# Moving seven pieces of w2 and the last turns of wq to later steps of a backward pass

## The chip, the cores and the metric

The kernel runs on one core of a Trainium2 chip. Its time is the device time of one execution in microseconds (us); three runs were timed, and their median is the figure compared. One more execution was recorded by the hardware profiler, and every duration below comes from that record.

The core has engines that work side by side and each take their own instructions in order: PE multiplies matrices (PEld loads its weights), DVE and ACT work on vectors, POOL does so too and issues some transfers, and SP here only issues transfers (DMAs). Sixteen DMA engines move the bytes between the chip's memory and the core's own.

## What is computed

Two transformer layers with the same weights, one token per sequence, two sequences, forward and backward. Each layer is an attention block over a cached K and V (4 heads of K and V, 16384 positions, 128 wide; 32 heads of queries) and an MLP with a layer norm in front of each:

```python
x = x + _A_ref(_layernorm(x), A_k_cache, A_v_cache, A_wq, A_wo)   # attention, layer 0
x = x + _B_ref(_layernorm(x), B_w1, B_b1, B_w2, B_b2)             # MLP, layer 0
x = x + _A_ref(_layernorm(x), A_k_cache, A_v_cache, A_wq, A_wo)   # attention, layer 1
x = x + _B_ref(_layernorm(x), B_w1, B_b1, B_w2, B_b2)             # MLP, layer 1
...
_out, _vjp = jax.vjp(_f, A_x, A_k_cache, A_v_cache, A_wq, A_wo, B_w1, B_b1, B_w2, B_b2)
_grads = _vjp(grad_out)
return (_out0, *[jnp.asarray(_g) for _g in _grads])
```

In the attention `q = x @ wq`, the scores are softmaxed, `o = p @ v`, and the result is `o @ wo`. In the MLP `y = _layernorm(x)`, `h = gelu(y @ w1 + b1)`, and the result is `h @ w2 + b2`. The outputs are the last x (`out_0`) and the gradients of x, of both caches (32 MB each, in bfloat16), of the four weights and of the two biases. w2 is 3584 x 1024.

## The kernel before

**The list of pieces.** The program isn't written engine by engine. Each small piece of work is a Python function that is put on one list with `emit`, together with the chunks of memory that it uses. At the end `Program.run` (L109) walks through the list in order and calls the functions; every engine then has its instructions in exactly that order. So the place of a piece in the list is its place in the order of each engine that it touches.

**Chunks and slots.** Whatever is loaded comes in chunks of up to 1 MB (128 partitions x 4096 numbers of 2 bytes), one DMA on SP each. Sixteen tiles called `slot`, and for a time a few others (halves of `e`, `ds` and `late`), hold chunks. `run` places chunks in the order of their first use, as soon as a slot is free that fits, often a dozen pieces ahead; a chunk keeps its slot until the last piece that uses it. SP issues its DMAs in that same order, and each waits until the slot's last user is done. A chunk may also be a scratch area of the program, without a load. `Program.keep` (L79) decides which chunks stay in their slot between two uses; after that there are 338 loads.

**The backward pass of layer 1.** `attn_bwd` (L1048) goes over the eight pairs of sequence and K/V head in order, 16 steps for each, 128 steps in all, and 14 more (`LAG_B`), in which only what lags behind is left. A step s does this:

- DVE turns a quarter of a V chunk (`kblock`, L554), and PE multiplies it with the gradient (L567), two steps later in the list. A chunk of V so lasts four steps.
- PE multiplies a quarter of a K chunk, 14 steps behind V's (`direct`, called as `pk`; L592), so the last K chunks are used at steps 126 to 141.
- Twice in 16 steps DVE makes the scores' gradient (`slope`, L1067 and L1070) and ACT and POOL exchange its parts (`exchange`, L602).
- Then come the pieces in `wb` and `extra` for that step.

`wb` holds the weights of the attention: wo's next group, and wq's group of the head just finished. The last group of wq is turned at steps 118 to 125, and its products (`tail`) come when the pass is over. To turn a piece in place (`turn_here`, L451), PE transposes eight blocks of 128 x 128 into PSUM (L457) and ACT copies them back over the piece (L460). `here_products` (L466, PE at L470) multiplies a turned piece.

`extra` holds the MLP's w2, which layer 1's forward result and layer 0's backward pass both need. It is loaded once, in seven chunks (pieces) of 512 rows. `w2_fwd_piece` (L892, PE at L896) makes 32 products with a piece as it was loaded, and then four `turn_here` turn it in place. It keeps its slot until the pass is over, when `here_products` uses it for layer 0. After the seventh piece `x_out` (L1451, two DVE additions) finishes x, and `col_to_row` (L626) makes it `out_0`: two PE transposes (L633), a DVE copy into a scratch chunk that lies in a load slot (L634), and a DMA of 4 KB on POOL (L635).

**After the pass**, in this order: the first of the transposes on DVE that turn w1 for layer 0 (`turn_rows`, L442), the eight products of the last wq group, the backward pass of the layer norm (`attn_in_bwd`, L1187; on DVE from L672 on, with one PE product at L683), more turns of w1, and the 28 products of w2 (L470). Their result is needed by everything of layer 0. Layer 0's backward pass also makes and stores the large outputs.

The lines around the change:

Of the kernel before, what the change touches and what calls it, by code (L numbers as in the profile page):

```python
# [182 lines left out]
def kernel(  # L183
# [70 lines left out]
    def ob():  # L254
        st["ob"] += 1
        return obanks[st["ob"] % len(obanks)]
# [139 lines left out]
    def ld_w2():  # L396
        return [ld_rows("w2", B_w2, 4 * i, 4, 0, D) for i in range(FJ // 4)]

    def col(c, j, n, o):
        return c.ap[:, j * n + o * 128:j * n + (o + 1) * 128]  # L400
# [83 lines left out]
    def turned_products(ps, t, w0, nw, vb, first, last, parts=1):  # L484

        def f(k):
            def fn():
                tv = t.ap[:, 0:nw * 256].rearrange("p (w x e) -> p w x e", x=128, e=2)
                for w in range(k * nw // parts, (k + 1) * nw // parts):
                    for e in range(2):  # L490
                        J = (w0 + w) // 2
                        PE.matmul(ps(), lhsT=tv[:, w, :, e], rhs=vb()[:, 2 * (w % 2) + e, :, 2 * J:2 * J + 2],
                                  start=(first and w == 0 and e == 0), stop=(last and w == nw - 1 and e == 1),
                                  skip_group_check=True)
            return fn

        return [(f(k), [t]) for k in range(parts)]
# [128 lines left out]
    def col_to_row(colT, dram_out, queue=None, kind="half"):  # L626
        c = P.chunk(kind=kind)

        def f():
            row = c.ap[0:DJ, 0:256].rearrange("p (b n) -> p b n", b=2)  # L630
            ps = ob()[0:DJ, 0:256].rearrange("p (b n) -> p b n", b=2)
            for b in range(2):
                PE.transpose(ps[:, b, :], colT[:, :, b], identf[:])  # L633
            V.tensor_copy(out=row, in_=ps)  # L634
            (queue or GP).dma_start(dram_out.rearrange("b (j n) -> j b n", n=128), row)  # L635

        return f, [c]
# [254 lines left out]
    def w2_fwd_piece(l, ws, i, fps):  # L892
        def f():
            for j in range(4):
                for o in range(DJ):
                    PE.matmul(fps[:, o, :], lhsT=col(ws[i], j, 1024, o), rhs=h_all[:, 4 * i + j, 2 * l:2 * l + 2],  # L896
                              start=False, stop=True, skip_group_check=True)
        return f, [ws[i]]
# [79 lines left out]
    def wo_bwd_ops(l, k, vb):  # L978

        acc = sb[0][:, 64:80].rearrange("p (c a b) -> p c a b", c=2, a=4)  # L980

        def fin():
            raw = regroup(acc, ob())
            V.memset(sb[0][:, 64:80], 0.0)
            dve(0.3)
            do_of(l, k, raw)

        return turned_pair(ld_wo(k), acc, vb), (fin, ())
# [10 lines left out]
    def wo_mid_ops(l, k):  # L999

        ws = ld_wo(k)
        ps = sb[0][:, 64:80].rearrange("p (r b) -> p r b", b=2)
        turns = [turn_here(ws[r // 4], (r % 4) * 1024, 8) for r in range(R)]
        prods = [here_products(ws[r // 4], (r % 4) * 1024, 8, lambda r=r: ps[:, r, :],
                               lambda o: gA_all[:, o, 2 * l:2 * l + 2], False) for r in range(R)]

        def fin():
            do_of(l, k, ps)
            V.memset(sb[0][:, 64:80], 0.0)
            dve(0.1)  # L1010

        saved["wo"] = ws
        return turns, prods, (fin, ())
# [13 lines left out]
    def wq_bwd_ops(l, k):  # L1027

        acc = sb[0][:, 96:112].rearrange("p (c a b) -> p c a b", c=2, a=4)
        hold = {}  # L1030

        def sp():
            vb, fn = spread(lambda: dq_all[:, k * R:(k + 1) * R, 2 * l:2 * l + 2], 8, "vg")
            hold["vb"] = vb
            fn()

        return [(sp, ())] + turned_pair(ld_wq(k), acc, lambda: hold["vb"]())

    def wq_last_ops(l, k):

        ws = ld_wq(k)
        ps = sb[0][:, 112:128].rearrange("p (j b) -> p j b", b=2)
        turns = [turn_here(ws[j // 4], (j % 4) * 1024, 8, "act" if l == 1 else None) for j in range(DJ)]
        prods = [here_products(ws[j // 4], (j % 4) * 1024, 8, lambda j=j: ps[:, j, :],
                               lambda r: dq_all[:, k * R + r, 2 * l:2 * l + 2], l == 0) for j in range(DJ)]
        return turns, prods

    def attn_bwd(l, order, gT, wo_first, outputs=None, mark=None, extra=None, after=()):  # L1048
# [9 lines left out]
        ev, wb = {}, {}  # L1058
# [33 lines left out]
        for pos, g in enumerate(order):  # L1092
            quick = l == 0 and pos == G - 1
            for f in range(2):
                n = 117 + 5 * f if quick else 16 * pos + 10 + 8 * f
# [10 lines left out]
        for i, k in enumerate(kvs):  # L1106
            if i + 1 < HKV and l == 1:
                turns, prods, fi = wo_mid_ops(l, kvs[i + 1])
                for n in range(8):
                    wb.setdefault(32 * i + 17 + n, []).append(turns[n])  # L1110
                    wb.setdefault(32 * i + 18 + n, []).append(prods[n])
                wb.setdefault(32 * i + 27, []).append(fi)
                turns, prods = wq_last_ops(l, k)
                for n in range(8):
                    wb.setdefault(32 * i + 24 + LAG_B + n, []).append(turns[n])
                    wb.setdefault(32 * i + 33 + LAG_B + n // 4, []).append(prods[n])
            elif i + 1 < HKV:
                ops, fi = wo_bwd_ops(l, kvs[i + 1], vba)
                for n, b in enumerate(ops + [fi]):
                    wb.setdefault(32 * i + 19 + n, []).append(b)  # L1120
                for n, b in enumerate(wq_bwd_ops(l, k)):
                    wb.setdefault(32 * i + 33 + LAG_B + n, []).append(b)
            else:
                if l == 0:
                    wb.setdefault(32 * i + 12 + LAG_B, []).append((dn_kept, ()))
                ops, tail = wq_last_ops(l, k)
                for n, b in enumerate(ops):
                    wb.setdefault((118 if l == 1 else 121) + n, []).append(b)

        kc, vc = {}, {}  # L1130
        n_steps = 128 + LAG_B if l == 1 else N_END
# [5 lines left out]
        s = 0  # L1137
        while s <= n_steps:
# [16 lines left out]
            n = -(-len(fill) // 3)  # L1155
# [3 lines left out]
            for v in v_at.get(s, ()):  # L1159
                pos, i = divmod(v, 16)  # L1160
# [253 lines left out]
    def mark(name):  # L1414
        def f(n=0):
            marks[name, n] = len(P.ops)
        return f
# [11 lines left out]
    def at_sb0(c0, n):  # L1429
        return sb[0][:, c0:c0 + n]  # L1430
# [20 lines left out]
    def x_out(xn, xT, fps):  # L1451
        V.tensor_tensor(out=xn[:], in0=fps, in1=b2T[:].to_broadcast([128, DJ, 2]), op=ALU.add)
        V.tensor_tensor(out=xn[:], in0=xn[:], in1=xT[:], op=ALU.add)
# [21 lines left out]
    xA1 = attn_fwd(1, down, lambda: xM0, mark("e1"), w1_turns[0:2], tw[5][1] + tw[6][0] + tw[6][1] + [(dh_last_, ())])  # L1475
# [29 lines left out]
    xM1 = vec.tile([128, DJ, 2], F32, name="xM1")  # L1505
    fps1 = at_sb0(288, 16).rearrange("p (j b) -> p j b", b=2)
    ws2b = ld_w2()
    extra = {2: [(lambda: V.memset(fps1, 0.0), ())]}
    for i in range(7):
        extra.setdefault(26 + 13 * i, []).append(w2_fwd_piece(1, ws2b, i, fps1))  # L1510
    extra[106] = [(lambda: x_out(xM1, xA1, fps1), ())]

    ws2c = ws2b
    dhps0 = at_sb0(160, 56).rearrange("p (j b) -> p j b", b=2)
    w2_turns = [turn_here(ws2c[j // 4], (j % 4) * 1024, 8) for j in range(FJ)]
    for n, b in enumerate(w2_turns):
        extra.setdefault(29 + 13 * (n // 4) + 3 * (n % 4), []).append(b)

    ws1c = [ld_rows("w1q", B_w1, 4 * h, 4, cg * 896, 896) for h in range(2) for cg in range(4)]
    dm_0 = quads(at_sb0(224, 16))  # L1520
# [2 lines left out]
    for n, c in enumerate(ws1c):  # L1523
        t = w1t[n // 4][n % 4] if n == 7 else P.chunk()
        t1 += [] if n == 7 else turn_rows(c, t, 896)
        p1 += turned_products(lambda n=n: dm_0[:, n // 4], t, 14 * (n % 4), 14, vh0, n % 4 == 0, n % 4 == 3)
    extra[111] = [col_to_row(xM1, out_0.rearrange("b s d -> (b s) d"), kind="load")]
    attn_bwd(1, up, lambda: saved["g3"], (None, wo_prods), mark=mark("d1"), extra=extra, after=t1[0:1])
    wo_prods0 = wo_first_ops(0, down[0] % HKV, saved["wo"])[2]

# [36 lines left out]
    extra = {4: [(spread_a0, ())]}  # L1567
# [22 lines left out]
    def outputs(s, rest=False):  # L1590
# [16 lines left out]
        return res  # L1607

    attn_bwd(0, down, lambda: saved["g1"], (va0, wo_prods0), outputs=outputs, extra=extra)
    slots = []  # L1610
    for i, t in enumerate(slot_tiles):
# [46 lines left out]
```

## Time and profile before

| | us |
|---|---|
| runs: median (lowest, highest) | 1102.76 (1102.6, 1106.79) |
| the profiled execution: its time | 1105.32 |
| its span, first to last instruction | 1103.5 |
| busy in the span: PE / DVE / ACT / POOL | 815.1 / 754.9 / 486.1 / 177.0 |
| layer 1's backward pass | 442 to 638 |
| moved in the span | 448.07 MB, 406 GB/s |

A line of the profile names an engine, a line of the kernel (L554), an operation and the tiles as out<-in; the number behind it is a duration or a busy time in us. Behind "<-" in square brackets stands how long the engine was idle before, and who ended that wait. "PEclk" and the third last column of a stretch are the share of its full clock that PE was granted. A DMA share of about 1 means that all sixteen DMA engines had packets throughout; it can come out slightly over 1.

### The profile page before, as it was taken

The numbers are of one execution on the slowest core, as the hardware profiler recorded it, in microseconds if no ns is written. First come the engines' busy times: TensorE is split into PE (matmuls) and PEld (weight loads), VectorE is DVE, ScalarE is ACT, GpSimd is POOL, SyncE is SP. The second block draws the span as 40 slices with busy tenths as digits, with TensorE's granted clock in tenths as the row PEclk, the third lists the DMA queues.
The fourth block names the chain that finished last, engine by engine and source line by source line (L and its number), as shares of the span: only waits on it lengthen the run. The fifth ranks groups of instructions, "written<-read, shape, count | busy, mean of one in ns | idle before, by whom it ended". The sixth has DMA issues, their size and how long they took to land. (4 is left out here: it accounts for less than half of the span.)

```text
span 1103.5 us, 34173 instructions
## 1 busy us (share of the span) xinstructions
PE 815.1 (74%) x14717; PEld 606.6 (55%) x14717; DVE 754.9 (68%) x1442; ACT 486.1 (44%) x1101; POOL 177.0 (16%) x550
## 2 busy tenths in 40 slices
PE   5664666457888657788788578887887897798885
PEld 4554565456777556678778564444443443344453
DVE  5864665168888627665646466887786895698874
ACT  0332222101243321245434426776675785577873
POOL 1000000001000000111111101323332332233330
PEclk9999999999999996588967757999897998899997
DMA  9999999999999999999999999999999999999996
GB/s 371 420 423 420 421 425 422 399 403 397 416 423 421 422 420 373 411 417 421 416 421 398 372 375 392 334 396 423 420 420 424 424 420 420 426 421 421 417 424 249
DMA packets 97404, 448.07 MB, mean 406 GB/s; under 512 B 7608, under 2 KB 11214, under 8 KB 58852
## 3 DMA queue, kind: packets, MB, share of 16 engines
q1 hardware_dynamic: 80004, 350.40, 77.9%
q0 software_dynamic: 17248, 95.48, 21.0%
q8 instruction: 115, 1.88, 0.6%
q14 instruction: 37, 0.30, 0.1%
HBM read 347.23 MB, written 98.62 MB: 404 GB/s over the span
## 5 line engine op out<-in xcount | busy, mean ns | idle before, releaser
L554 DVE STREAM_TRANSPOSE kT<-slot 128x512 int32<-128x512 int32 x432 | 292.0, 695 | 114.6 <-PE sc L567 92.0
L567 PE MATMUL sc<-qbd,kT 128*128 128x32 bf16 x4096 | 262.4, 222 | 14.5 <-DVE kT L554 10.2
L567 PEld LDWEIGHTS <-kT 128*128 128x128 bf16 x4096 | 208.4, 115 | 65.8 <-issue 34.2
L276 ACT CAST slot<-sc 128x512 bf16<-128x512 f32 x291 | 165.7, 593 | 81.0 <-PE sc L1337 44.1
L592 PEld LDWEIGHTS <-slot 128*128 128x128 bf16 x3424 | 140.0, 103 | 100.9 <-issue 49.6
L592 PE MATMUL sb<-xt,slot 128*128 128x8 bf16 x3424 | 156.2, 177 | 41.9 <-DMA slot<-in_A_v_cache_dram 22.9
L1277 PE MATMUL sc<-slot,late 128*128 128x512 bf16 x338 | 128.6, 403 | 28.9 <-DVE slot L279 12.6
L279 DVE CAST slot<-sc 128x512 bf16<-128x512 f32 x166 | 111.6, 678 | 25.4 <-PE sc L1277 12.3
L787 ACT ACTIVATE e<-sc 128x512 bf16<-128x512 f32 x32 | 19.0, 597 | 236.3 <-DVE sc L784 168.9
L460 ACT COPY slot<-tp 128x512 int32<-128x512 int32 x92 | 52.7, 587 | 113.6 <-PE tp L457 91.3
L276 ACT CAST slot<-sb 128x512 bf16<-128x512 f32 x139 | 82.3, 592 | 25.1 <-PE sb L1337 13.4
L457 PE MATMUL tp<-ident,slot 128*128 128x128 bf16 x800 | 74.9, 255 | 11.9 <-DMA slot<-in_A_wq_dram 8.9
L1277 PEld LDWEIGHTS <-late 128*128 128x128 bf16 x512 | 44.9, 99 | 64.7 <-issue 52.3
L1337 PE MATMUL sc<-slot,late 128*128 128x512 bf16 x170 | 66.0, 407 | 16.9 <-DVE slot L279 9.6
L602 ACT COPY xt<-e 32x128 int32<-32x128 int32 x256 | 75.6, 295 | 3.9
L1277 PE MATMUL sb<-slot,late 128*128 128x512 bf16 x174 | 70.3, 404 | 9.5 <-DVE slot L279 3.7
L279 DVE CAST slot<-sb 128x512 bf16<-128x512 f32 x88 | 59.7, 678 | 15.9 <-PE sb L1277 7.1
L457 PEld LDWEIGHTS <-slot 128*128 128x128 bf16 x800 | 60.7, 116 | 14.4 <-DMA slot<-in_A_wq_dram 7.3
L442 DVE STREAM_TRANSPOSE slot<-slot 128x1024 int32<-128x1024 int32 (+1 forms) x44 | 51.0, 1184 | 15.6 <-DMA slot<-in_A_wo_dram 7.5
L602 POOL COPY xt<-ds 32x64 int32<-32x64 int32 x128 | 29.7, 232 | 178.6 <-DVE ds L1070 119.8
L662 POOL TENSOR_TENSOR m_rstd<-ln_vpe,neghalf 128x2 f32<-128x2 f32 x2 | 1.4, 720 | 350.3 <-DVE ln_vpe L660 350.3
L602 POOL COPY xt<-late 32x64 int32<-32x64 int32 x240 | 55.5, 231 | 13.1 <-DVE late L1070 1.6
(292 smaller groups left out, 1074.5 us busy)
## 6 DMA issues: line engine op xcount, KB each, us to landing
slot<-in_A_k_cache_dram SPq DMA_DIRECT2D x102, 1024.0 KB, 15.4
slot<-in_A_v_cache_dram SPq DMA_DIRECT2D x100, 1024.0 KB, 17.3
out_dram<-slot POOLq DMA_DIRECT2D x55, 1024.0 KB, 15.1
slot<-in_A_wq_dram SPq DMA_DIRECT2D x26, 1024.0 KB, 17.5
slot<-in_A_wo_dram SPq DMA_DIRECT2D x25, 1024.0 KB, 17.7
out_dram<-slot POOLq DMA_DIRECT2D x40, 512.0 KB, 16.5
slot<-in_B_w_dram SPq DMA_DIRECT2D x21, 896.0 KB, 15.9
slot<-in_B_w_dram SPq DMA_DIRECT2D x12, 1024.0 KB, 13.9
```

Of the source, the lines that this page charges most:

```text
L276: S.copy(out=dst, in_=src)
L279: V.tensor_copy(out=dst, in_=src)
L442: V.transpose(out=t.ap[:, h * nw * 256:(h + 1) * nw * 256].bitcast(I32).rearrange("p (w j m) -> p w j m", j=4, m=32), in_=c.ap[:, 0:4 * nc ...
L457: PE.transpose(tp[:, j * 128:(j + 1) * 128], c.ap[:, off + j * 128:off + (j + 1) * 128], ident[:])
L460: S.copy(out=d.bitcast(I32), in_=tp.bitcast(I32))
L554: V.transpose(out=kT[:].bitcast(I32).rearrange("p (w j m) -> p w j m", w=4, j=4), in_=c.ap[:, (i % 4) * 1024:(i % 4 + 1) * 1024].bitcast(I ...
L567: PE.matmul(sc[:, a0:a0 + 4, :, 2 * (i % 4) + q], lhsT=kv[:, 2 * q + w, :, e], rhs=qbd[:, q_at(g), 2 * w + e], start=(w == 0 and e == 0), ...
L592: PE.matmul(acc, lhsT=c.ap[:, n * 128:(n + 1) * 128], rhs=xv[:, i // 4, t // 2, :, 2 * (i % 4) + t % 2], start=(fresh and i == 0 and t == ...
L602: (GP.tensor_copy if on[t % len(on)] == "g" else S.copy)(out=d[32 * t:32 * t + 32, c0:c0 + cn, j, :], in_=s[32 * j:32 * j + 32, c0:c0 + cn ...
L787: S.activation(out=e_of(l, g)[:, 8 * f:8 * f + 8].rearrange("p a h b -> p h a b"), in_=sc[f][:].rearrange("p h (a b) -> p h a b", b=8), fu ...
L1277: PE.matmul(ps, lhsT=hold["blk"][:, j, :], rhs=flat(qm(w)[:, hf * 4:hf * 4 + 4, :]), start=True, stop=True)
L1337: PE.matmul(ps, lhsT=hold[j // 4 * 4][:, j % 4, :], rhs=Y.ap[:, y_at + c0:y_at + c0 + cn], start=True, stop=True)
```

## The change

The seven pieces of w2 had their products at steps 26, 39, 52, 65, 78, 91 and 104, and each piece's four turns 3, 6, 9 and 12 steps after them. Now the products are at steps 44, 60, 76, 92, 106, 118 and 130, and the turns 2, 4, 6 and 8 steps after them. `x_out` moves from step 106 to 132, `col_to_row` for `out_0` from 111 to 137. The last wq group is turned at steps 126 to 133 instead of 118 to 125. Nothing is added or left out; as chunks are placed by their first use, the order of the loads and the slots that they get follow.

```diff
                 ops, tail = wq_last_ops(l, k)
                 for n, b in enumerate(ops):
-                    wb.setdefault((118 if l == 1 else 121) + n, []).append(b)
+                    wb.setdefault((126 if l == 1 else 121) + n, []).append(b)
...
-    for i in range(7):
-        extra.setdefault(26 + 13 * i, []).append(w2_fwd_piece(1, ws2b, i, fps1))
-    extra[106] = [(lambda: x_out(xM1, xA1, fps1), ())]
+    w2_at = (44, 60, 76, 92, 106, 118, 130)
+    for i, s_ in enumerate(w2_at):
+        extra.setdefault(s_, []).append(w2_fwd_piece(1, ws2b, i, fps1))
+    extra.setdefault(132, []).append((lambda: x_out(xM1, xA1, fps1), ()))
...
-        extra.setdefault(29 + 13 * (n // 4) + 3 * (n % 4), []).append(b)
+        extra.setdefault(w2_at[n // 4] + 2 * (1 + n % 4), []).append(b)
...
-    extra[111] = [col_to_row(xM1, out_0.rearrange("b s d -> (b s) d"), kind="load")]
+    extra[137] = [col_to_row(xM1, out_0.rearrange("b s d -> (b s) d"), kind="load")]
```

## The prediction

> **What bounds the kernel now.** I read first the page's forty slices. The DMA row is at 9 almost throughout, so for most of the span the kernel moves bytes as fast as its queues allow; time can be won or lost only where that row dips, or where a chain of computation makes the transfers wait.
>
> ```profile
> DMA  9999999999999999999999999999999999999996
> GB/s 371 420 423 420 421 425 422 399 403 397 416 423 421 422 420 373 411 417 421 416 421 398 372 375 392 334 396 423 420 420 424 424 420 420 426 421 421 417 424 249
> ```
>
> The change touches layer 1's backward pass (442 to 638 us) and what hangs on its end. So next the busy time by stretches; the last two columns are the DMA engines' share and GB/s.
>
> ```profile
> 442.00:600.00 158.00, 124.58 (x2837) 117.42 (x2835) 96.00 (x187) 65.11 (x175) 24.16 (x104) 0.76 1.02 418
> 600.00:613.00 13.00, 9.62 (x266) 9.13 (x265) 8.96 (x16) 5.42 (x15) 2.54 (x9) 0.89 0.75 270
> 613.00:636.00 23.00, 14.43 (x304) 13.85 (x304) 8.39 (x14) 8.47 (x24) 3.71 (x16) 0.72 1.02 419
> ...
> 646.00:650.00 4.00, 3.03 (x89) 2.83 (x87) 1.80 (x4) 0.00 (x0) 0.00 (x0) 0.50 0.57 169
> 650.00:685.00 35.00, 29.66 (x458) 19.15 (x455) 22.27 (x45) 19.27 (x37) 4.03 (x6) 0.63 1.02 414
> 685.00:720.00 35.00, 30.93 (x327) 15.60 (x327) 30.64 (x50) 26.93 (x52) 13.90 (x43) 0.95 0.89 320
> 720.00:1085.00 365.00, 302.57 (x3693) 163.62 (x3692) 286.89 (x479) 251.10 (x489) 117.36 (x337) 0.92 1.01 419
> ```
>
> The DMA engines are full up to 600, lose 13 x 0.25 = 3.25 us in 600:613, are full again, lose 4 x 0.43 = 1.7 us in 646:650, and 35 x 0.11 = 3.9 us in 685:720, where DVE and PE are busy 31 of 35 us: there computation sets the pace. After 720 the transfers do.
>
> What empties the queues at 600:613? SP's own waits (560 to 740 us) hold this line, and the timeline shows the event:
>
> ```profile
> SPq L383 <- DMA out_dram<-slot: 7.1, 1, 7.1
> ```
>
> ```profile
> 603.99 0.38 PE L633 MATMUL sc<-identf,xM 128*8 128x128 f32 x2
> ...
> 604.46 0.41 DVE L634 CAST slot<-sc 8x256 bf16<-8x256 f32 x1 [1.26 <-PE sc L633]
> ...
> 605.17 0.68 POOL L635 DMA_DIRECT2D out_dram<-slot x1 [9.21 <-DVE slot L634]
> ...
> 610.71 0.38 SPq L383 DMA_DIRECT2D slot<-in_A_wq_dram  x1
> ```
>
> At step 111 the row of out_0 is built in a load slot (PE, DVE) and stored by POOL. The next load on SP, a half of the last wq group, goes into that slot, and waits until the 4 KB store has landed: 605.17 + 5.5 = 610.7. Five more loads stand behind it on SP. That is 2.5 of the 3.25 us; the rest (600 to 602.5) follows from PE's two waits at steps 104 and 106, the first two lines here:
>
> ```profile
> 590.68 0.95 PE L896 MATMUL sb<-h_all,slot 128*128 128x2 bf16 x32 [1.52 <-DMA slot<-in_B_w_dram]
> ...
> 595.75 1.03 PE L457 MATMUL tp<-ident,slot 128*128 128x128 bf16 x8 [1.86 <-DMA slot<-in_A_wq_dram]
> ...
> 597.24 1.90 PE L457 MATMUL tp<-ident,slot 128*128 128x128 bf16 x16
> ...
> 636.76 1.02 PE L592 MATMUL sb<-xt,slot 128*128 128x8 bf16 x32 [1.18 <-DMA slot<-in_A_k_cache_dram]
> ```
>
> The last line is the pass's last K chunk arriving: 636.76. From it the tail runs on DVE:
>
> ```profile
> 637.82 0.18 DVE L1077 TENSOR_SCALAR dq_all<-sb 128x8 bf16<-128x8 f32 x1 [5.38 <-PE sb L592]
> ...
> 638.97 1.11 DVE L442 STREAM_TRANSPOSE slot<-slot 128x896 int32<-128x896 int32 x1 [0.83 <-DMA slot<-in_B_w_dram]
> 640.08 0.17 DVE L672 TENSOR_TENSOR lb_dr<-sb,a_rstd 128x16 f32<-128x16 f32 x1
> ```
>
> The norm's backward begins at 640.08, behind the first transpose of w1, and everything of layer 0 follows from it.
>
> **The change, part by part.** Sums are made against this profiled execution (1105.32 us: span 1103.5 and 1.8 around it; 2.6 above the median of 1102.76). Only differences are used, and put onto the median.
>
> *Loads.* 338 planned loads and their bytes stay. The n-th load is released by the same step's work in both kernels (read from the two programs, loads 181 to 255); only which chunk it brings changes, K and V coming up to three places sooner, w2 11 to 18 places later. No byte is saved, so a gain can come only from the lull of 3.25 us. I take all of it as gone: the wait at 595.75 falls away (its wq half comes three places, 7.5 us, sooner), and SP no longer stops behind out_0. One load of 1 MB is 2.5 us at 419 GB/s. So the last K chunk, the same place in the queue as before, arrives at 636.76 - 3.25 = 633.5; w2's seventh piece, now two places ahead of it, at 628.5. Were nothing of the lull saved, both are 3.25 later.
>
> *PE at the end.* 224 products of w2 and 224 transposes with 28 ACT copies move later, and 64 transposes with 8 copies (wq) by 8 steps; none is added. Up to step 129 they lie beside waits for loads (PE 14.43 of 23 us busy in 613:636): at nothing; without that cover a piece costs 0.95 + 4 x 0.5 to 0.95. But step 130's products of the seventh piece stand in PE's order ahead of all the rest, and cannot start before 628.5. Behind them, up to out_0's transposes at step 137: the products 0.95; seven groups on K (1.02 for four, 0.21 each) 1.5; six turns (three of wq, three of w2); out_0's two transposes 0.39. A turn is 0.95 at the slow clock (597.24: two in 1.90), 0.53 at the fast one (two in 1.06 at 587.21). Sum 6.0 to 8.5; end 634.5 to 637.0. The granted clock was 0.72 in 613:636, in the middle; I take 7.3, so 635.8. ACT's copies (0.59 each, two PSUM banks) keep up beside the one exchange of 2.05; x_out's two DVE additions of about 0.17 are free, since DVE idles 5.38 there.
>
> *out_0's store.* The built order of the changed kernel puts out_0's row into the slot that the first transpose of w1 (L442, DVE) writes next, and that transpose now waits for the store; the norm's backward stands behind it on DVE. From PE's end to the landing: 0.08 + 0.41 + 0.30 to POOL's issue, + 5.5 = 6.3; + 1.11 for the transpose: 7.4. POOL has nothing ahead of it (its last exchange ends about 629). The norm begins at 634.5 + 7.4 = 641.9 to 644.4; mid 643.2. Before: 640.08. So +1.8 to +4.3, mid +3.1. wq's eight product groups (1.85 us on PE, 638.19) end before that.
>
> The store's 5.5 us is one row, taken while the DMA engines were 0.5 to 1.0 busy. [...]
>
> *Behind the norm.* One w1 quarter now takes the slot of w2's first piece and is issued some 2.9 us after the norm begins (was 639.2). It is used 12.5 us after; a load into an empty queue landed in 4.7 (433.9 to 438.6), the page's median for this kind is 15.9 behind a full queue. The queue is dry by then: at nothing, at worst +6. The second lull grows by about 4 us; as computation sets the pace until 720, that costs nothing more, and the +3.1 passes through to the end one for one.
>
> *Bounds.* Below: PE keeps up fully, so that only the chunk before the last (631.0) and 0.85 + 0.39 of PE stand ahead: 632.2 + 7.4 = 639.6, -0.4. Above: the lull isn't saved and the clock is slow: 631.8 + 8.5 + 7.4 = 647.7, +7.6.
>
> **The rivals.**
> *Faster: the lull is the whole of it.* If the first transpose did not have to wait on the store, the tail starts with the last K chunk and the gain is 3.25: 1099.5. It decides if out_0's transposes end by 636.8 - 7.4 = 629.4. For: DVE idles 5.38 us before the tail. Against: the seventh piece itself comes at 628.5, and the store's semaphore is in that transpose's waits. 0.13.
> *Much slower: PE held by its own order.* w2's fifth, sixth and seventh pieces are needed at steps 106, 118 and 130, just as they land; PE can't pass them, falls behind, slots come free late and the lull stays: +7.6, 1110.4. For: PE waited at 590.68 for just such a piece. Against: the loads are released some 12 us ahead. 0.20.
> *The store lands quickly.* At best it has landed when POOL's 0.68 us issue ends: 4.8 less than in my sum, so -1.7: 1101.1. For: 4 KB are a two-hundred-fiftieth of a load's 2.5 us. Against: the only such store took 5.5, and its end fell into an emptying queue; here loads are in flight. 0.10. [...]
> *No effect at the end:* computation's slack in 685:720 (4 of 35 us) swallows the delay: 1102.8 or so. 0.07.
>
> **How the numbers follow.** Forecast +3.1: 1105.9, chance 0.50, with its own range 1104.5 to 1107.1. For 8 in 10 I reach towards both sides: 1100.5 (half of the faster case out) to 1109.5 (half of the much slower out). A measurement of this kernel tells about 0.5% (5.5 us) from no change. Faster by more than that needs more than the whole lull: 0.04. Slower, past 1108.3: most of the 0.20 and a tail of the forecast, less what of that case stays below: 0.20. Within: 0.76.
>
> **What would show it.** Right: 600:613 at a DMA share near 1.0; no SP wait on out_dram there; DVE's L442 after dq_all waiting about 4 us for DMA out_dram; the last K chunk used near 633.5 or soon after (PE late); the norm (L672) at about 643; a longer second lull. Wrong: L442 not waiting for the store, that store landing well under 5.5 us, or PE waiting long at L896 with a lull still in front of it.

## The result and the profile after

The changed kernel is slower by about a third of a per cent: 1108.62 us (median of 22 runs, 1104.04 to 1112.95) against 1105.22 for the kernel before on the same chip (22 runs, 1102.6 to 1108.26). The ratio is 1.0030, its 95% interval 1.0021 to 1.0039, so +3.4 us. The forecast was +3.1 on a base of 1102.76, which is +0.28%. The base itself moved by 2.5 us between the two measurements, which is why the median lies nearer to the upper end of the range than the ratio does.

The profiled execution took 1104.04 us (span 1102.3). It is the shortest of the 22, 4.6 below their median, and shorter than the profiled execution of before (1105.32). What it lacks is found below; for now it shows what happens up to 650 us. First the busy time by stretches, with the granted clock of PE, the DMA engines' share and GB/s at the end of each line.

```profile
600.00:613.00 13.00, 9.98 (x236) 9.49 (x233) 8.76 (x14) 3.69 (x11) 2.53 (x11) 0.67 1.02 420
613.00:636.00 23.00, 18.09 (x388) 17.37 (x386) 6.08 (x14) 12.66 (x31) 3.68 (x14) 0.74 1.00 396
636.00:646.00 10.00, 5.78 (x200) 5.63 (x198) 6.20 (x14) 1.90 (x1) 0.00 (x0) 0.63 0.59 198
646.00:650.00 4.00, 2.24 (x78) 2.10 (x76) 1.25 (x3) 0.00 (x0) 0.15 (x1) 0.50 1.04 377
650.00:685.00 35.00, 31.24 (x474) 20.16 (x474) 23.13 (x47) 19.86 (x38) 4.38 (x7) 0.63 1.02 409
685.00:720.00 35.00, 30.92 (x353) 16.20 (x352) 31.54 (x52) 27.43 (x53) 14.72 (x44) 1.00 0.85 324
```

The lull of 600:613 is gone (share 0.75 before, 1.02 now), and SP's waits no longer hold a line on out_dram. In exchange the second lull has grown: 636:646 has a share of 0.59, which is 4.1 us without transfers, after 1.7 us (in 646:650) before. SP issues a load at 636.33 and the next one only at 642.88; it waits for PE's products behind the norm (two such waits, 10.8 us together, this one 6.1):

```profile
SPq L383 <- PE sb L470: 10.8, 2, 6.1
```

The timeline of the changed kernel shows why the norm, and PE behind it, are no earlier:

```profile
628.22 0.95 PE L896 MATMUL sb<-h_all,late 128*128 128x2 bf16 x32 [1.37 <-DMA late<-in_B_w_dram]
...
633.35 0.38 PE L633 MATMUL sc<-identf,xM 128*8 128x128 f32 x2
```

```profile
633.77 0.41 DVE L634 CAST slot<-sc 8x256 bf16<-8x256 f32 x1 [3.30 <-PE sc L633]
635.04 0.17 DVE L1077 TENSOR_SCALAR dq_all<-sb 128x8 bf16<-128x8 f32 x1 [0.86 <-PE sb L592]
...
639.07 1.11 DVE L442 STREAM_TRANSPOSE slot<-slot 128x896 int32<-128x896 int32 x1 [3.71 <-DMA out_dram<-slot]
```

```profile
634.48 0.68 POOL L635 DMA_DIRECT2D out_dram<-slot  x1 [5.02 <-PE tp L457]
```

PE waits for w2's seventh piece until 628.22 and then works without a gap; out_0's row comes out at 633.35, POOL sends its store off at 634.48, and DVE's first transpose of w1 stands 3.71 us until that store has landed at 639.07. The norm's backward follows at 640.10 (640.08 before).

### The profile page after: what moved, and what is told of

Read it like the earlier page. It is cut to its first block, busy times and chain, and to the rows that moved or that the text cites. A ratio compares the mean times of both kernels' runs of the same rounds, so it can differ in the third digit from the quotient of the medians.

```text
span 1102.3 us, 34166 instructions
## 1 busy us (share of the span) xinstructions
PE 824.2 (75%) x14717; PEld 615.7 (56%) x14717; DVE 753.9 (68%) x1442; ACT 487.0 (44%) x1101; POOL 176.1 (16%) x550
## 5 line engine op out<-in xcount | busy, mean ns | idle before, releaser
L567 PE MATMUL sc<-qbd,kT 128*128 128x32 bf16 x4096 | 268.5, 224 | 14.8 <-DVE kT L554 11.1
L567 PEld LDWEIGHTS <-kT 128*128 128x128 bf16 x4096 | 213.2, 117 | 63.2 <-issue 31.4
L592 PE MATMUL sb<-xt,slot 128*128 128x8 bf16 x3488 | 160.4, 177 | 42.4 <-DMA slot<-in_A_v_cache_dram 24.5
L460 ACT COPY slot<-tp 128x512 int32<-128x512 int32 x84 | 48.6, 586 | 103.8 <-PE tp L457 87.8
L457 PE MATMUL tp<-ident,slot 128*128 128x128 bf16 x736 | 72.6, 261 | 2.2 <-DMA slot<-in_A_wq_dram 1.7
L442 DVE STREAM_TRANSPOSE slot<-slot 128x1024 int32<-128x1024 int32 (+1 forms) x46 | 52.7, 1178 | 15.3 <-DMA slot<-in_A_wq_dram 5.9
```

The lines of the kernel that those rows point to most:

```text
L442: V.transpose(out=t.ap[:, h * nw * 256:(h + 1) * nw * 256].bitcast(I32).rearrange("p (w j m) -> p w j m", j=4, m=32), in_=c.ap[:, 0:4 * nc ...
L457: PE.transpose(tp[:, j * 128:(j + 1) * 128], c.ap[:, off + j * 128:off + (j + 1) * 128], ident[:])
L460: S.copy(out=d.bitcast(I32), in_=tp.bitcast(I32))
L567: PE.matmul(sc[:, a0:a0 + 4, :, 2 * (i % 4) + q], lhsT=kv[:, 2 * q + w, :, e], rhs=qbd[:, q_at(g), 2 * w + e], start=(w == 0 and e == 0), ...
L592: PE.matmul(acc, lhsT=c.ap[:, n * 128:(n + 1) * 128], rhs=xv[:, i // 4, t // 2, :, 2 * (i % 4) + t % 2], start=(fresh and i == 0 and t == ...
```

## The experiments

All ratios are to the kernel before, run beside each kernel on the same chip. Where the row is built "in the corner", a small function of its own replaces `col_to_row`; it makes the same row in an unused corner of the long-lived tile `late`, so that no load slot is tied to the store. In these kernels the function shifts what follows by 12 lines (L684 there is L672 here, L1089 is L1077):

```diff
+            row = Lt[0:8, 4096:4352].rearrange("p (b n) -> p b n", b=2)
+            ps = ob()[0:DJ, 0:256].rearrange("p (b n) -> p b n", b=2)
+            for b in range(2):
+                PE.transpose(ps[:, b, :], colT[:, :, b], identf[:])
+            V.tensor_copy(out=row, in_=ps)
+            GP.dma_start(dram_out.rearrange("b (j n) -> j b n", n=128), row)
```

### The wait for the store, taken out of the changed kernel

```diff
-    extra[137] = [col_to_row(xM1, out_0.rearrange("b s d -> (b s) d"), kind="load")]
+    extra[137] = [col_to_row_own(xM1, out_0.rearrange("b s d -> (b s) d"))]
```

> The changed kernel with one edit: out_0's row is built in a corner of the tile late (columns 4096 to 4351) that nothing else uses in this pass, instead of a load slot, so no load and no transpose waits for the store. Store theory (the transpose of w1 that stands ahead of the norm on DVE waits for out_0's store): the changed kernel's 3.71 us wait goes, the norm then follows wq's products, about 2.8 us sooner; ratio to the kernel before 0.997 to 1.000, and no DVE wait for out_dram. Rival (PE is held by w2's late pieces, the wait on the store is only where the delay shows): the time stays that of the changed kernel, 1.002 to 1.004.

1103.86 us, ratio 0.9991 (0.9979 to 1.0002). Against 1.0030 (and 1.0040 for the changed kernel in its second measurement, below) taking the store out of the load slot is worth 0.4 to 0.5%, 4.3 to 5.4 us. DVE's lines in this kernel:

```profile
636.58 0.41 DVE L646 CAST late<-sc 8x256 bf16<-8x256 f32 x1 [4.54 <-PE sc L645]
637.85 0.18 DVE L1089 TENSOR_SCALAR dq_all<-sb 128x8 bf16<-128x8 f32 x1 [0.86 <-PE sb L592]
638.10 0.07 DVE L1091 MEMSET sb<- 128x8 f32 x1
638.14 1.11 DVE L442 STREAM_TRANSPOSE slot<-slot 128x896 int32<-128x896 int32 x1
640.06 0.17 DVE L684 TENSOR_TENSOR lb_dr<-sb,a_rstd 128x16 f32<-128x16 f32 x1 [0.81 <-PE sb L470]
```

The transpose (L442) now follows 0.3 us after the query gradient. But this is no kernel of 1099.5 us, as the rival "the lull is the whole of it" had it for this case: something else eats most of the lull's 3 to 4 us. Nor do the profiles show 4 us at the norm: it begins at 640.06 here, since PE had the slow clock ahead of the row (0.54 and 0.61 in 632:634 and 634:636, 1.00 in both for the changed kernel's first profile), at 640.10 in the changed kernel's first profile and at 641.20 in its second, below. Where the rest of the gain arises is taken up in the section on the prediction.

### The same corner in the kernel before

```diff
-    extra[111] = [col_to_row(xM1, out_0.rearrange("b s d -> (b s) d"), kind="load")]
+    extra[111] = [col_to_row_own(xM1, out_0.rearrange("b s d -> (b s) d"))]
```

> The kernel before with the same one edit: out_0's row at step 111 in the corner of late. Store theory: SP's 7.1 us wait goes, the lull of the DMA engines at 609 to 613 (2.5 us lost) goes, the last K chunk arrives 2.5 us sooner and so does all behind it: ratio 0.9975, between 0.996 and 0.999. Rival (the lull was not on the path, computation ends the pass): 1.000.

1101.21 us, ratio 0.9966 (0.9954 to 0.9978). SP's queue no longer waits for out_0's store, and 600:613 is nearly full:

```profile
600.00:613.00 13.00, 9.75 (x274) 9.14 (x271) 9.14 (x16) 6.02 (x16) 2.52 (x9) 0.89 0.97 372
```

So the edit that removes this lull is worth 3.7 us, and it is one call, with no piece of work moved. At the norm its profile shows 1.7 us (638.35 after 640.08), a second one, below, 2.8 (637.26).

### Each half of the change alone

First w2 alone: the changed kernel with wq's turns put back.

```diff
-                    wb.setdefault((126 if l == 1 else 121) + n, []).append(b)
+                    wb.setdefault((118 if l == 1 else 121) + n, []).append(b)
```

> w2's pieces, x_out and out_0 at the new steps, wq's last turns back at steps 118 to 125. The planner then gives out_0's row another slot, which nothing takes again before the norm, so nothing on the path waits for the store. Store theory: no DVE wait for out_dram ahead of the norm, and the gain of the lull shows: 0.996 to 0.999. Rival (w2's pieces at 106, 118 and 130 hold PE): they are still there, so 1.002 to 1.004.

1102.69 us, ratio 0.9983 (0.9971 to 0.9994). With wq's turns back in their place the row falls into another load slot, which nothing on the path takes before the norm (L672 at 638.5): no wait for the store, and half of the 0.34%.

The other half (the kernel before, 126 for 118):

> Only wq's last turns moved to steps 126 to 133; w2, x_out and out_0 stay at the old steps. Store theory: SP still waits for out_0's store at step 111 with a load behind it, the tail has no wait on it: 0.999 to 1.001. Rival (it is wq's turns at 126 to 133 that make the pass end late): 1.002 or more.

1108.83 us, ratio 1.0034 (1.0017 to 1.0050). This was a miss: it was expected to be no change. The lull and its wait are both still there, and behind them the wq halves come late, and PE stands for them:

```profile
SPq L378 <- DMA out_dram<-slot: 7.3, 1, 7.3
```

```profile
628.11 1.04 PE L457 MATMUL tp<-ident,slot 128*128 128x128 bf16 x8 [2.09 <-DMA slot<-in_A_wq_dram]
```

The last products with K then end about 1.5 us later than before (query gradient at 639.3, before 637.8), and the norm starts at 641.6 (640.1). This profiled execution took 1105.43 us, hardly more than that of before and 3.4 less than the median here, so it doesn't show where the median loses its 0.34%.

### Do the late turns of wq cost without the lull?

The kernel before with the row in the corner, and 126 for 118:

> The kernel before, with out_0's row built in a corner of the long-lived tile `late` instead of a load slot, and the last group's wq turns at steps 126 to 133. It asks where the +0.34% of the wq turns alone came from. Theory: the late turns cost only because the wq halves arrive behind the lull, when SP has waited for out_0's store; without that wait the halves come some 3 us sooner and the turns lie beside other work: ratio to the kernel before 0.9955 to 0.9980, the norm (L672) at 638 to 639.5. Rival: eight turns close to the end of the pass hold PE by themselves, whatever the loads do: 0.9990 to 1.0010, the norm at 640 or later.

1106.59 us, ratio 1.0014 (1.0001 to 1.0027), 0.48% above the same kernel with the turns at 118. The theory holds at the norm, which starts at 638.1, no later than with the early turns (638.35), and fails in the time; the rival is nearly right in the time and fails at the norm. In the profiles most of the loss lies 50 us further on, in the first stage of layer 0 that computation paces:

```profile
685.00:720.00 35.00, 30.13 (x284) 14.93 (x284) 27.80 (x45) 24.34 (x47) 13.43 (x42) 0.85 0.69 260
```

The DMA engines lose 11 of 35 us here; with the early turns the line of the same stretch reads:

```profile
685.00:720.00 35.00, 30.91 (x352) 16.23 (x349) 31.40 (x52) 26.74 (x50) 14.15 (x43) 1.00 0.95 346
```

What differs with them is PE's granted clock, 0.85 against 1.00. In steps of half a microsecond it is 0.50 from 697.8 to 708, right after PE has waited for DVE, which had waited for a store of 512 KB or 1 MB:

```profile
696.88 0.69 DVE L279 CAST slot<-sb 128x512 bf16<-128x512 f32 x1 [2.26 <-DMA out_dram<-slot]
```

```profile
697.62 0.58 PE L1289 MATMUL sb<-slot,late 128*128 128x512 bf16 x1 [2.71 <-DVE slot L279]
```

With the early turns the same two waits are 0.79 and 1.25 us, and no drop follows. The last two sections come back to this.

### The row four steps later, in another slot

```diff
-    extra[137] = [col_to_row(xM1, out_0.rearrange("b s d -> (b s) d"), kind="load")]
+    extra.setdefault(141, []).append(col_to_row(xM1, out_0.rearrange("b s d -> (b s) d"), kind="load"))
```

> The changed kernel with out_0's row at step 141 instead of 137. The row then lands in another load slot, which nothing on the path takes before the norm, though the store itself goes out about 1 us later. Theory (the wait of the first w1 transpose for the store is what the change costs): no wait on out_dram ahead of the norm, some 4 us less than the changed kernel, ratio to the kernel before 0.9980 to 1.0000. Rival (the late row, or PE's late end, costs by itself): 1.0020 to 1.0050, as the changed kernel.

1105.98 us, ratio 1.0017 (1.0004 to 1.0029). Between the two: 0.23% better than the changed kernel beside it, not the 0.4% expected. In its profile DVE does not wait for the store at all (L442 at 638.41), but DVE's order holds the row's copy (637.80) ahead of the query gradient, and PE reaches the row late, at 637.39: it stands four steps later, and PE had the slow clock on the way (0.50 in 630:634; turns of 1.01 us, 0.61 in the changed kernel's first profile). The norm starts at 640.34. As its profile reads, moving the row takes the store's wait away and pays part of that back in PE's late end.

### The seventh piece of w2 earlier, and all combinations

With the row in the corner, so that no kernel waits for that store, w2's pieces at three sets of steps were combined with two places of wq's turns.

```diff
-    w2_at = (44, 60, 76, 92, 106, 118, 130)
+    w2_at = (44, 60, 76, 90, 100, 110, 118)
```

(with `x_out` at 120 and the row at 123)

> The changed kernel with out_0's row in the corner of `late`, and w2's pieces at steps 44, 60, 76, 90, 100, 110, 118 instead of 44, 60, 76, 92, 106, 118, 130 (x_out at 120, the row at 123). It asks what the 0.25% is by which the changed kernel stays behind the kernel before when both build the row in that corner. Theory: PE held behind the seventh piece at step 130; with that piece 12 steps sooner the ratio to the kernel before is 0.9960 to 0.9980. Rival: it is the wq turns at 126 to 133, or a different order of loads: about 0.9990 as with the pieces late.

> out_0's row in the corner of `late`, w2's pieces at steps 44 to 118, the wq turns back at 118 to 125. With the kernels run so far it fills a table of three places of w2 by two places of wq, all without a wait for out_0's store. Theory: the wq turns at 126 to 133 cost nothing at the end of the pass; where they cost 0.48% (with w2's pieces early) the loss lay behind the pass, in 685 to 720, and this kernel stands where it stands with the late turns: ratio 0.9960 to 0.9980. Rival: the late turns always cost, so without them this is faster still: 0.9920 to 0.9955.

> The changed kernel with out_0's row in the corner of `late` and the wq turns back at 118 to 125: w2's late pieces alone, without the store's wait. Theory (PE is held behind the seventh piece at step 130, whatever the wq turns do): 0.9980 to 1.0000. Rival (it was the wq turns behind that piece): 0.9955 to 0.9975, as with the pieces at 44 to 118.

> The kernel before with out_0's row in the corner of `late`, once more, beside the other two on the same chip, since it had five runs: 0.9955 to 0.9980, and a second profile of the stretch 685 to 720. If PE's wait there is under 1.5 us again, the granted clock stays at 1.00 behind it; in the ten profiles so far it fell to 0.50 behind every wait of 1.6 us or more and behind none that was shorter.

Ratios to the kernel before (95% interval):

| w2's seventh piece at step | wq turned at 118 to 125 | wq turned at 126 to 133 |
|---|---|---|
| 104 (as before) | 0.9966 (0.9954 to 0.9978), again 0.9959 (0.9944 to 0.9975) | 1.0014 (1.0001 to 1.0027) |
| 118 | 0.9963 (0.9952 to 0.9974) | 0.9969 (0.9958 to 0.9980) |
| 130 (as in the change) | 0.9980 (0.9968 to 0.9992) | 0.9991 (0.9979 to 1.0002) |

Two things follow. The seventh piece at 130 instead of 118 costs 0.17% with one place of wq and 0.22% with the other, about 2 us; the first pair's intervals overlap, the second's just meet. That it costs this by holding PE is argued, not shown: with the early wq turns the norm begins at 638.72 and 638.74 in the two profiles, with the late ones 0.9 us later (640.06 and 639.16). At 118 instead of 104, beside early turns, it costs nothing that the runs can tell. The late turns of wq cost 0.06 and 0.11% beside late pieces, less than the intervals can tell, and 0.48% beside early ones. So their price is no sum of its own; it depends on the rest of the plan. Why just that combination meets the longest wait at 697 stays open. The fastest kernels (0.9959 to 0.9966; medians 1100.57 to 1101.21 us) beat both the kernel before and the changed one, and the simplest of them moves nothing but out_0's row out of the load slot.

### The changed kernel once more

> The changed kernel once more, beside the other three on the same chip, and for a second profile: ratio to the kernel before 1.0020 to 1.0045. The first profile had the fast clock in the last 8 us of the pass and PE's end at 633.7. If the end of PE goes with the granted clock, as the sum had it, a profile with the slow clock there has out_0's transposes end at 635 to 637 and the norm at 641.5 to 643.5; the wait of the first w1 transpose for out_0's store is 3.5 to 5 us in either.

1108.54 us, ratio 1.0040 (1.0026 to 1.0055); the profiled execution took 1107.92, near its median.

```profile
634.91 0.41 DVE L634 CAST slot<-sc 8x256 bf16<-8x256 f32 x1 [3.31 <-PE sc L633]
...
640.16 1.11 DVE L442 STREAM_TRANSPOSE slot<-slot 128x896 int32<-128x896 int32 x1 [3.66 <-DMA out_dram<-slot]
641.20 0.13 DVE L672 TENSOR_TENSOR lb_dr<-sb,a_rstd 128x16 f32<-128x16 f32 x1
...
650.93 0.22 DVE L1544 SCALAR_TENSOR_TENSOR dh_all<-sb,nslope 128x56 bf16<-128x56 f32 x1 [2.69 <-PE sb L470]
```

The wait for the store is the same (3.66; 3.71), all else about 1.1 us later: PE got w2's seventh piece at 629.35, not 628.22. PE's turns there were at the fast clock again (1.00 in 630:636; 0.61 us), so the slow case that was asked for has not been seen in this kernel. Its timeline has a wait that is followed by a drop of the clock, and the stretches from 700 on show it:

```profile
699.00 0.38 PE L1277 MATMUL sb<-slot,late 128*128 128x512 bf16 x1 [2.21 <-DVE slot L279]
```

```profile
700.00:705.00 5.00, 5.00 (x44) 2.57 (x41) 3.43 (x6) 3.44 (x7) 0.55 (x1) 0.58 0.89 331
705.00:710.00 5.00, 4.92 (x39) 2.27 (x37) 4.10 (x7) 3.48 (x7) 0.72 (x1) 0.74 0.52 215
```

The changed kernel's first profile has a clock of 1.00 in both stretches, at a wait of 1.48. The next section shows that 2.7 of the 3.9 us between the two executions arise here.

## Why the prediction was right, step by step

**The lull: right.** It was taken as 3.25 us, wholly gone. The share of 600:613 is 1.02, and the kernel before without it is faster by 0.34%, again 0.41% (3.7 and 4.5 us).

**PE at the end: right in its mechanism, too long in its size.** The seventh piece was put at 628.5 (it came at 628.22 and 629.35), and out_0's transposes behind its products and six turns at 634.5 to 637.0, with 635.8 taken. In the two profiles they end at 633.7 and 634.9. From the piece's products to that end are 5.5 us in both, less than the 6.0 to 8.5 of the sum, at the fast clock (1.00 from the piece's products to that end; turns of 0.61 us, the next work starting 0.44 after each). Where the clock dropped in between, as in the changed kernel with the row in the corner (0.54 in 632:634), it was 6.75 us, and they ended at 636.5.

**out_0's store: right in its mechanism, too long in its size.** DVE's L442 waits for out_dram as forecast, 3.7 us (about 4). From issue to landing it took 634.48 to 639.07, 4.6 us, and 4.5 in the second profile; the sum had 5.5, from the one such store in the trace of before. From PE's end to the landing is 5.3 us instead of 6.3. Both terms together put the norm at 640.1 and 641.2 instead of 643.2.

**Behind the norm: this step failed.** It said that the norm's delay passes to the end one for one, and that nothing else is added: "as computation sets the pace until 720, that costs nothing more". The norm was delayed by 0.0 and 1.1 us, not 3.1, and yet the medians differ by 3.4. Nor did what delay there was reach the end one for one. Three places behind the norm show it.

The first is on PE. Between the norm and `dh_all`, the result of w2's products, lie 8.85 us before, but 9.79 and 9.73 in the changed kernel. Near the end of those products PE pauses for nothing that the profile shows, 0.66 us before and 1.56 in the second profile of the changed kernel:

```profile
650.41 0.48 PE L470 MATMUL sb<-gM_all,late 128*128 128x2 bf16 x12 [1.56 <-issue]
```

So `dh_all` is 1.0 and 2.0 us late. The late load of w1 that had been priced at nothing was not the cause: no wait for it appears.

The second is the products of `dh_all` with w1 (L492), whose result DVE takes up in `uq` (L540). In them it is the kernel before that pauses for nothing shown (its two lines stand first below); the changed kernel has no such pause above 0.25 us. So the first `uq` comes at 662.20 before, and at 661.58 and 662.62 in the changed kernel's two profiles. Of the 2.0 us at `dh_all` 0.4 are left.

```profile
655.63 0.57 PE L492 MATMUL sb<-kT,slot 128*128 128x8 bf16 x16 [0.92 <-issue]
...
661.80 0.36 PE L492 MATMUL sb<-kT,slot 128*128 128x8 bf16 x8 [1.12 <-issue]
```

```profile
662.62 0.22 DVE L540 TENSOR_TENSOR uq<-sb,quad 128x64 f32<-128x64 f32 x1 [1.98 <-PE sb L492]
```

The third is the clock in 697 to 708. From `dh_all` on DVE has the same instructions in the same order in all kernels, so two of them can be used as marks: the first `uq`, and the second, some 74 us later. The table has for all thirteen profiles when `dh_all` and the first `uq` are made, the longest wait of PE in 684 to 703, how long the clock was then at 0.50, and the time from the first `uq` to the second.

| kernel | dh_all | first uq | PE's wait | at 0.50 | uq to uq | time |
|---|---|---|---|---|---|---|
| before | 648.93 | 662.20 | 1.61 | 3.4 | 74.40 | 1105.32 |
| changed | 649.89 | 661.58 | 1.48 | 0 | 73.32 | 1104.04 |
| changed, again | 650.93 | 662.62 | 2.21 | 6.8 | 76.01 | 1107.92 |
| changed, row in the corner | 649.89 | 661.86 | 1.43 | 0 | 73.26 | 1103.86 |
| before, row in the corner | 647.27 | 659.72 | 1.25 | 0 | 73.29 | 1101.84 |
| the same, again | 646.22 | 659.49 | 1.21 | 0 | 73.25 | 1101.42 |
| w2 alone | 648.35 | 660.54 | 1.00 | 0 | 72.79 | 1101.49 |
| wq alone | 651.95 | 663.91 | 1.23 | 0 | 72.85 | 1105.43 |
| wq alone, row in the corner | 648.65 | 660.88 | 2.71 | 10.2 | 77.62 | 1107.69 |
| row at 141 | 650.07 | 662.31 | 1.78 | 3.4 | 75.07 | 1106.00 |
| w2 to 118, wq at 126, corner | 649.28 | 662.02 | under 0.4 | 0 | 72.23 | 1102.75 |
| w2 to 118, wq at 118, corner | 648.68 | 660.64 | under 0.4 | 0 | 72.19 | 1101.76 |
| w2 to 130, wq at 118, corner | 648.42 | 661.19 | under 0.4 | 0 | 72.23 | 1102.49 |

From the second `uq` to the last instruction lie 366.4 to 367.5 us in all thirteen, so a profile's time is decided before that. Between the two marks lie 72.2 to 73.3 us where the clock doesn't fall, 74.4 and 75.1 where it is at 0.50 for 3.4 us, 76.0 for 6.8 and 77.6 for 10.2. The changed kernel's two profiles are of one and the same program, and this stretch is 2.7 of the 3.9 us between them. Beside the profile of before, the changed kernel's second one has lost 0.4 us at the first `uq`, 1.6 more at the second, and 0.6 behind it: 2.6 us in all, where the medians differ by 3.4.

Lateness alone doesn't make PE's wait there long: wq alone is the latest at the first `uq` and waits 1.23 us, and wq alone with the row in the corner is 3 us earlier and waits 2.71. Whether the change makes these waits longer in most of its runs can't be told from two profiles, and stays open.

By runs the parts of the change can be told apart, whatever their way to the end. The kernel before without the lull's wait stands at 0.9966; with w2 at the late steps too, at 0.9980; with wq's turns late as well, at 0.9991; and with the row in the load slot again, which is the changed kernel, at 1.0030 and 1.0040. So the lull's gain is lost to the late pieces, 0.25%, and to the row's slot, 0.4 to 0.5%. The sum of +3.1 had both causes, but it came out near +3.4 partly by luck: the norm's delay was put 2 to 3 us too high, and what follows the norm was put at nothing.

**The rivals.** "The lull is the whole of it" needed the store off the path; with the row in the corner the changed kernel reached 0.9991, not the 0.9971 that 1099.5 stands for; with the seventh piece 12 steps sooner as well, it does (0.9969). "PE held by its own order" had the lull stay, and it went; that the late seventh piece costs about 2 us is a term of the result and not its whole. "The store lands quickly" is half a truth: 0.9 to 1.0 us quicker, not 4.8. What was held against it, loads in flight, was no more here than before: 281 and 269 GB/s moved beside the store, 288 before. "No effect" is excluded by the interval.

## What to carry to other kernels

Here a store of 4 KB cost more than a load of 1 MB (2.5 us at 419 GB/s), since its scratch sat in a slot that the next instruction of a queue or an engine needed: SP stood 7.1 us for it in the kernel before, DVE 3.7 us in the changed one. Give such rows a place of their own before moving work around them; that alone gave 0.34 to 0.41%, and no order of the rest that was tried gave more. A delay on the path is not finished where it was made: follow it by marks that both kernels have, down to the place from which their times run alike, and see what it does to waits and to the clock on the way. And where executions of one kernel spread by up to 9 us (1104.04 to 1112.95), compare medians for the verdict, and read a profile only together with where its own time stands among them.

## What the hardware showed that was not expected

- PE's clock after short waits. In the thirteen profiles the clock dropped to 0.50 in 697 to 708 in the four where PE's longest wait in 684 to 703 was 1.61 us or more (1.61, 1.78, 2.21, 2.71), behind that wait, and in none of the nine where it was 1.48 or shorter, and it stayed there for 3.4, 6.8 or 10.2 us; the drop began up to about 2 us after the wait. That the waits cause the falls was read from the profiles, not tested.
- The pause of PE with no cause shown, in the same products of w2 with the norm's gradient: 0.66 to 0.74 us in the three profiles with w2 and wq in the places of before, 1.49 to 2.19 in the ten others. What makes it longer stays open; eight of the thirteen profiles have further pauses of the kind (0.33 to 1.12 us) in the products with w1 that follow.
- The landing of a 4 KB store from POOL, from issue to landing, went with what the DMA engines moved meanwhile: 2.9 us at 112 GB/s (row at 141), 4.5 to 4.6 at 204 to 281 (five profiles, the changed kernel's two among them), 5.5 and 5.7 at 288 and 284 (before and wq alone, where the queues ran dry at the end), and 5.0 to 6.0 at 357 to 414 (five profiles). No run varied this alone.
